# q and k loaded as runs of 18 tokens, with scores of 128 rows of contraction, and the first two weight tiles in two transfers ahead of v

## The chip, the cores and the metric

The kernel runs on one core of one Trainium2 chip. The core has TensorE (PE in the profile; its weight loads are PEld), VectorE (DVE), ScalarE (ACT), GpSimd (POOL) and SyncE (SP), and 16 DMA engines that all queues share. The metric is the time of one execution on the device in microseconds, the median over several executions.

## The reference

The inputs are q, k, v of shape (8, 8, 576, 64), that is batch, heads, tokens and head size, gates s of shape (8, 8, 576), and the weights w_r and w_i (64, 512, 512) and w_ch (512, 512), all in float32. First comes causal attention with a bias from the cumulative sum of the gates:

```
scores = q @ k.T / sqrt(64)
cum    = cumsum(max(s, 0))                      # along the tokens
scores = where(key after query, -1e9, scores + min(-(cum[query] - cum[key]), 0))
attn   = softmax(scores);   x = attn @ v        # heads side by side: (8, 576, 512)
```

Then a mixing of the first 64 frequencies along the tokens, with one complex 512x512 matrix to each frequency, and a last product:

```
X  = rfft(x, axis=tokens)
Yr = Xr[m] @ w_r[m] - Xi[m] @ w_i[m]
Yi = Xr[m] @ w_i[m] + Xi[m] @ w_r[m]            # m = 0 .. 63, zero above
u  = x + irfft(Y)
out = u + max(u @ w_ch, 0)
```

The two weight tensors hold 64 x 512 x 512 numbers each, 134 MB together, and each number is read once.

## The kernel before

**Work items.** The attention runs over N = 32 items. Item n is a pair of heads g = n // 8 (two of the eight heads) in a batch b = n % 8. A loop over n at the end of the attention part makes one pass for each item. In pass n, PE does in this order: the scores of head h = 0 of item n (`scores(n, 0)`), the second head's product of probabilities and v for item n - 1 (`av(n - 1, 1)`), the first part of the transposes of item n + 1 (`transposes(n + 1, 0)`), `scores(n, 1)`, `transposes(n + 1, 1)`, the forward transform of item n - 1 (`fft(n - 1)`), `av(n, 0)`, and the products with weight tiles that are due (`modes`). From pass 26 on, six passes also do parts of the last product ahead of time. The order is written out by hand; each engine takes its instructions in that order and waits on semaphores.

**Loads.** All loads of q, k, v and the weights go through POOL's queue, by `nc.gpsimd.dma_start` in `load` (L226), and turn float32 into 16 bits on the way. Eight semaphores serve POOL's transfers in turn, so each issue waits until the eighth transfer before it has landed. In pass n, `load` mixes the four transfers of item n + 3 (q, k, and v for two heads; `LA = 3`) with the weight transfers of this pass; each list is spread evenly over the pass. How many weight tiles a pass loads is planned ahead (`on_chip`), so that a tile is only loaded into a buffer whose last use was in an earlier pass. A weight tile covers 4 frequencies by 128 rows by 512 columns and is loaded by two transfers of 256 KB (at the destination), each to 64 of the 128 partitions, with runs of 2 KB. The first eight tiles lie in space that is used for something else later (`early`); the rest go round two rings of 11 and 6 buffers. Counted over the passes, passes 12, 14, 16, 20, 26 and 28 load no or one weight tile, most others 4 or 5.

**q and k.** A tile of q holds both heads of an item. Its 128 partitions are (head, 64 groups), and a group is a run of R = 9 tokens of 64 numbers: 2304 B at the source, 1152 B at the destination. k has a tile of its own. Each pool entry is one item; there are four (`bufs=LA + 1`).

**Transposes.** `transposes(n, 0)` turns q of item n and `transposes(n, 1)` turns k. Each makes 18 PE transposes of 64x64 (9 token positions, two heads) into one PSUM tile `tr_ps`, of which there is one. Head 0 comes out on partitions 0 to 63 and head 1 on 64 to 127. Two copies (L336) take them to SBUF: `qtA`, `qtB` by DVE; `ktA` by DVE and `ktB` by ACT. Tiles A have 65 rows (64 of the head and one for the cumulative sum of the gates, row 64 of q against a row of ones in k). Tiles B have 128 rows: the extra row is row 0, rows 1 to 63 are zeros, and the head is in rows 64 to 127. There are two sets, for even and odd items. SP brings the row of cumulative sums of each item and head (`cum_rows`, two small transfers an item).

**Scores.** For each head and each of two key residues, PE writes the causal mask into PSUM (L368), adds keys times queries (L374; contraction over 65 rows for h = 0, over 128 for h = 1), and ACT takes the exponential (L382). The last 64 tokens are handled for both heads together in `scores4` (L345, L349).

**Start.** Before the loop, SP loads s, two constants and, a little later, three more constants; POOL loads q and k of item 0, and then three weight tiles mixed with v of item 0, the last 64 tokens' v (`loads_tails`), and q, k, v of item 1. DVE sets the fixed rows of the tiles, casts the identity and the mask, and makes the cumulative sums; PE's first transposes come after that.

**End.** After the loop, `loads_w(len(wq))` issues the remaining weight tiles. PE multiplies each as it lands (L452), with parts of the last product between. After the last tile come the inverse transform, the last product, and the results' way out.

## Time and profile before

| What | Value |
|---|---|
| median of 6 executions | 447.95 us (447.44 to 448.89) |
| the profiled execution's own time | 448.01 us |
| its span, first to last instruction | 446.1 us |
| PE busy | 357.6 us (80%) |
| POOL busy | 259.8 us (58%) |
| DVE busy | 251.3 us (56%) |
| ACT busy | 218.7 us (49%) |
| DMA packets | 77251, 93.30 MB, mean 209 GB/s |
| q transfers | 32 of 144 KB, median 7.2 us to landing |
| k transfers | 32 of 144 KB, median 7.0 us to landing |
| v transfers | 72 of 64 KB, median 6.9 us to landing |
| weight transfers | of 256 KB, median 8.0 us to landing |

How to read it: the profile shows one execution. The page cuts the span into 40 slices of 11.15 us; in each slice a digit is the busy share of an engine in tenths, PEclk is TensorE's granted clock in tenths of full speed, and GB/s counts the bytes at the destination of the transfers. Most loads read 4 bytes and write 2, so what is read from HBM is nearly twice that. The chain that ended last is followed back from the last instruction, at each step to what released it. A wait line names who waited, for whom, and then the total in microseconds, how many times, and the longest. A timeline line has the start, the time it took, the engine, line and operation, and in brackets the idle time before it with what ended that. A window line has the stretch, its length, each engine's busy time with the number of instructions, the granted clock, the DMA engines' share and GB/s. The share sums the packets' own times, and since packets of one engine overlap, a full stretch shows more than 1.

### The profile page before, as it was taken

The page shows a single profiled execution, that of the slowest core. Times are in us where ns is not written, and L with a number is a line of the kernel's source. Part 1 is how long each engine was busy: PE and PEld are TensorE (multiplying, and loading weights), DVE is VectorE, ACT ScalarE, POOL GpSimd, SP SyncE. Part 2 cuts the span into 40 slices and gives each one's busy share as a digit, 9 for nine tenths or more (in the row PEclk, how much of TensorE's full clock was granted, in tenths as well). Part 3 has the DMA queues.
Part 4 walks back from the last instruction along what each step waited for, and adds up shares of the span by engine and source line. Part 5 has one row for each costly group of instructions (what it writes and reads, how often), then busy time and mean ns, then how long its engine had stood idle before and what let it go on. Part 6 is the DMA issues. An engine that isn't in the chain of part 4 may idle for free.

```text
span 446.1 us, 11492 instructions
## 1 busy us (share of the span) xinstructions
PE 357.6 (80%) x4729; PEld 222.5 (50%) x4729; DVE 251.3 (56%) x576; ACT 218.7 (49%) x387; POOL 259.8 (58%) x405
## 2 busy tenths in 40 slices
PE   1788998998476989957868976779987997769994
PEld 0466665566244666634545544546654555333341
DVE  6777676477243476644436455446665554441885
ACT  1486876177224474734436345556550344221583
POOL 7866765755566666555565656566543544440393
PEclk9999998699665699986669869889998899979999
DMA  9999999999999999999999999999999999996598
GB/s 178 199 203 205 205 202 206 201 207 206 207 207 203 195 190 199 208 207 207 206 200 206 207 207 206 208 205 203 206 210 211 209 210 209 209 217 131 173 351 346
DMA packets 77251, 93.30 MB, mean 209 GB/s; under 512 B 30144, under 2 KB 39872, under 8 KB 77200
## 3 DMA queue, kind: packets, MB, share of 16 engines
q0 software_dynamic: 67984, 81.29, 105.4%
q1 hardware_dynamic: 9216, 11.29, 7.8%
q8 instruction: 37, 0.61, 0.5%
q14 instruction: 14, 0.11, 0.1%
HBM read 163.51 MB, written 9.44 MB: 388 GB/s over the span
## 4 chain that ended last, share of the span: by engine, by line
DMA 68%; PE 14%; issue 6%; POOL 6%; DVE 4%; POOLq 1%; ACT 0%; DVEq 0%
DMA w_sb<-in_moe_w_i_dram 38%; DMA w_sb<-in_moe_w_r_dram 14%; DMA q<-in_q_dram 8%; PE sc_ps L374 3%; POOL r_w L766 3%; PE av_ps L403 2%; PE ft_ps L429 2%; PE sc_ps L368 2%; PE tr_ps L333 2%; DMA wch_sb<-in_moe_w_ch_dram 2%; DMA y_acc<-in_moe_w_r_dram 2%; DMA v<-in_v_dram 2%; DMA y_acc<-in_moe_w_i_dram 1%; DMA x_all<-in_moe_w_r_dram 1%; PE yp L452 1%
## 5 line engine op out<-in xcount | busy, mean ns | idle before, releaser
L382 ACT ACTIVATE p_sb<-sc_ps,cumt_sb 128x576 f16<-128x576 f32 (+1 forms) x256 | 142.0, 636 | 60.5 <-PE sc_ps L374 60.0
L226 POOL DMA_DIRECT2D w_sb<-in_moe_w_r_dram x120 | 71.6, 597 | 59.5 <-DMA w_sb<-in_moe_w_r_dram 19.8
L226 POOL DMA_DIRECT2D w_sb<-in_moe_w_i_dram x120 | 71.3, 596 | 46.9 <-DMA w_sb<-in_moe_w_i_dram 15.4
L226 POOL DMA_DIRECT2D v<-in_v_dram x72 | 51.7, 719 | 25.3 <-DMA w_sb<-in_moe_w_i_dram 7.5
L368 PE MATMUL sc_ps<-negm,ident 128*128 128x256 bf16 x256 | 56.1, 305 | 0.2
L452 PE MATMUL yp<-w_sb,xs 128*32 128x512 bf16 (+1 forms) x480 | 43.3, 441 | 9.4 <-DMA w_sb<-in_moe_w_i_dram 2.8
L333 PE MATMUL tr_ps<-ident,q 64*64 64x64 bf16 x576 | 17.0, 208 | 35.9 <-DMA q<-in_q_dram 35.9
L403 PE MATMUL av_ps<-v,p_sb 128*128 128x65 f16 x1024 | 44.9, 199 | 0.0
L374 PE MATMUL sc_ps<-qtB,ktB 128*128 128x512 bf16 (+2 forms) x192 | 43.6, 344 | 0.0
L336 DVE COPY ktA<-tr_ps 64x576 bf16<-64x576 bf16 x32 | 24.0, 749 | 33.0 <-PE tr_ps L333 33.0
L336 DVE COPY qtA<-tr_ps 64x576 bf16<-64x576 bf16 x32 | 23.8, 744 | 31.9 <-PE tr_ps L333 31.8
L403 PEld LDWEIGHTS <-p_sb 128*128 128x128 f16 x1024 | 39.0, 101 | 5.3 <-DVE x_all L413 2.3
L353 ACT ACTIVATE p<-sc_ps,cumt 128x64 f16<-128x64 f32 x32 | 10.1, 314 | 56.1 <-PE sc_ps L349 56.1
L374 PE MATMUL sc_ps<-qtA,ktA 65*128 65x512 bf16 (+2 forms) x192 | 37.1, 303 | 0.6 <-DMA qtA<-ncum_sb 0.6
L439 DVE CAST xs<-ft_ps 64x128 bf16<-64x128 f32 x128 | 31.4, 284 | 9.3 <-PE ft_ps L429 8.8
L429 PE MATMUL ft_ps<-Ff_sb,x_all 128*64 128x96 f16 (+1 forms) x640 | 34.1, 229 | 1.0 <-DVE x_all L413 1.0
L408 DVE TENSOR_REDUCE den<-av_ps 128x5 f32<-128x10 f32 x64 | 10.8, 169 | 41.6 <-PE av_ps L403 40.8
L452 PEld LDWEIGHTS <-xs 128*32 128x32 bf16 (+1 forms) x512 | 19.7, 146 | 27.7 <-issue 17.6
L413 DVE TENSOR_TENSOR x_all<-av_ps,rcp 128x320 f16<-128x320 f32 x64 | 31.5, 492 | 2.2
L333 PEld LDWEIGHTS <-q 64*64 64x64 bf16 x576 | 13.2, 120 | 38.5 <-DMA q<-in_q_dram 37.3
L336 ACT COPY ktB<-tr_ps 64x576 bf16<-64x576 bf16 x32 | 20.3, 634 | 22.2 <-DVE ktA L336 21.2
L333 PE MATMUL tr_ps<-ident,k 64*64 64x64 bf16 x576 | 16.9, 206 | 16.9 <-DVE qtB L336 8.1
(119 smaller groups left out, 558.7 us busy)
## 6 DMA issues: line engine op xcount, KB each, us to landing
w_sb<-in_moe_w_r_dram POOLq DMA_DIRECT2D x120, 256.0 KB, 8.0
w_sb<-in_moe_w_i_dram POOLq DMA_DIRECT2D x117, 256.0 KB, 8.1
out_dram<-r_w SPq DMA_DIRECT2D x14, 512.0 KB, 2.9
q<-in_q_dram POOLq DMA_DIRECT2D x32, 144.0 KB, 7.2
k<-in_k_dram POOLq DMA_DIRECT2D x32, 144.0 KB, 7.0
v<-in_v_dram POOLq DMA_DIRECT2D x72, 64.0 KB, 6.9
x_all<-in_moe_w_i_dram POOLq DMA_DIRECT2D x6, 256.0 KB, 6.8
out_dram<-r_w SPq DMA_DIRECT2D x6, 256.0 KB, 3.2
```

What stands on the lines that cost most here:

```text
L226: nc.gpsimd.dma_start(out=dst, in_=src)
L333: nc.tensor.transpose(ps[rows, r, :], src[rows, r, :], ident16[rows, rows])
L336: copy(out=dst[n % NQ][rows, :].rearrange("d (p r) -> d p r", r=R), in_=ps[rows].rearrange("d r p -> d p r"),)
L368: nc.tensor.matmul(ps[:, bass.ds(w * S, W)], ident16, negm[:, bass.ts(r, W)], start=True, stop=False, skip_group_check=True,)
L374: nc.tensor.matmul(ps[:, c0 : c0 + i1 - i0], keys[:, w, r, :], qt[:, i0:i1], start=False, stop=True, skip_group_check=True,)
L382: nc.scalar.activation(out=pt[:, poff[x] : poff[x] + S - w * W], in_=ps[:, w * S : (w + 1) * S - w * W], func=ACTF.Exp, bias=cumt_sb[:, x, ...
L403: nc.tensor.matmul(ps[:, I, r : r + NCH], lhsT, rhs, start=(i == 0), stop=(i == len(todo) - 1), skip_group_check=True,)
L413: nc.vector.tensor_tensor(out=x_all[:, g, b, :, D * h : D * h + D], in0=ps[:, :, 1 : NCH], in1=rcp.unsqueeze(2).to_broadcast([P, NT, D]), ...
L429: nc.tensor.matmul(ps[HP * h : HP * h + HP, q_, :], x_all[:nT, g, b, T, q_::2], Ff_sb[:nT, T, 3 * HM * h : 3 * HM * (h + 1)], start=(T == ...
L439: nc.vector.tensor_copy(out=xs[g % 2][rows, :, k, h, :, b, :], in_=ps[rows, :, k * HM : (k + 2) * HM].rearrange("p q (r m) -> p q r m", r=2),)
L452: nc.tensor.matmul(ps[32 * cg : 32 * cg + 32, :], cols[k0:, q_, 1 - ri, :, c * MC // 2 + cg], wt[(g, c, ri, cg // 2)][k0:, 2 * (cg % 2) + ...
L766: nc.gpsimd.tensor_tensor(out=rs[i], in0=rs[i], in1=z1s[i], op=ALU.add)
```

## The change

**q and k.** A run is now R = 18 tokens (RP = 32 groups), 4608 B at the source and 2304 B at the destination. One tile holds q on partitions 0 to 63 (two heads of 32 groups) and k on partitions 64 to 127, for two items, n and n + 1 (batches b and b + 1). One transfer brings q of both items and another k of both; for items 0 and 1 there is a transfer for each. There are two pool entries of two items. `loads_qk(n + LA)` is called in odd passes only, for items n + 3 and n + 4; `loads_v(n + LA)` in every pass.

**Transposes and tiles.** `transposes(n, half)` takes 9 of the 18 token positions of q and of k together, again in 18 PE transposes of 64x64. q comes out on rows 0 to 63 and k on rows 64 to 127, for both heads. The copies go to `qt` and `kt`, which have 128 rows and both heads side by side: 64 rows of the head, row 64 for the cumulative sum (ones in `kt`), and zeros below. DVE makes three of the four copies of an item and ACT the second half of k. The copies now write pieces of 9 elements and leave out 9.

**Scores.** Both heads contract over 128 rows.

**Start.** The first two weight tiles, which lie side by side, are loaded by two transfers of 512 KB at the destination (1 MB at the source) that stand between q and k of item 0 and v of item 0. The third weight tile is mixed with v of item 0, q and k of item 1, v of item 1 and the tails.

The diff, cut to its core:

```diff
-    R = S // (P // 2)
-    RP = P // 2
+    RP = P // 4
+    R = S // RP
+    RH = R // 2
...
-    qkpool = at.enter_context(tc.tile_pool(name="qk_sb", bufs=LA + 1))
+    qkpool = at.enter_context(tc.tile_pool(name="qk_sb", bufs=2))
...
-    qtA = [ap_.tile([NCH, S], BF16, name=f"qtA{i}") for i in range(NQ)]
-    qtB = [ap_.tile([P, S], BF16, name=f"qtB{i}") for i in range(NQ)]
+    qt = [ap_.tile([P, 2, S], BF16, name=f"qt{i}") for i in range(NQ)]
...
-    def loads_qkv(n):
+    def loads_qk(n):
...
-        q2 = qkpool.tile([P, R + 1, D], BF16, name="q2", tag="q2")[:, :R, :]
-        k2 = qkpool.tile([P, R + 1, D], BF16, name="k2", tag="k2")[:, :R, :]
+        t = loaded[n] = loaded[n + 1] = qkpool.tile([P, 2, R * D], BF16, name="qk2", tag="qk2")
+        return [
+            (
+                t[HP * i : HP * i + HP, x0:x1],
+                src[b + x0 : b + x1, hs].rearrange("b h (p r) d -> (h p) b (r d)", r=R),
+            )
+            for x0, x1 in ([(0, 2)] if n else [(0, 1), (1, 2)])
+            for i, src in enumerate((q, k))
         ]
...
+    def loads_v(n):
...
     def loads_w(upto):
         todo = []
+        if not wt:
+            t = y_acc[:, 2:6, :].rearrange("p c e -> p (c e)").bitcast(BF16)
+            for i in range(2):
+                wt[wq[i]] = early[i]
+            for h in range(2):
+                todo.append((
+                    t[HP * h : HP * h + HP].rearrange("p (m q e) -> p m (q e)", q=2, e=DM),
+                    moe_w_r[h : MC : 2, :P, :].rearrange("m (p q) e -> p m (q e)", q=2),
+                ))
...
-    first, second, tails0 = loads_qkv(0), loads_qkv(1), loads_tails(0)
+    first = loads_qk(0)
     load(first[:2])
-    load(loads_w(W0), first[2:] + tails0 + second)
+    load(loads_w(2))
+    load(loads_v(0) + first[2:] + loads_v(1) + loads_tails(0), loads_w(W0))
...
-        nc.vector.memset(qtB[i][0:64, :], 0.0)
-        nc.vector.memset(ktB[i][0:64, :], 0.0)
-        nc.vector.memset(ktB[i][0:1, :], 1.0)
-        nc.vector.memset(ktA[i][D : D + 1, :], 1.0)
+        nc.vector.memset(qt[i][D:], 0.0)
+        nc.vector.memset(kt[i][D:], 0.0)
+        nc.vector.memset(kt[i][D : D + 1], 1.0)
...
-        nc.sync.dma_start(out=qtA[n % NQ][D : D + 1, :], in_=ncum_sb[p0 : p0 + 1, :])
-        nc.sync.dma_start(out=qtB[n % NQ][0:1, :], in_=ncum_sb[p0 + 1 : p0 + 2, :])
+        for h in range(2):
+            nc.sync.dma_start(out=qt[n % NQ][D : D + 1, h, :], in_=ncum_sb[p0 + h : p0 + h + 1, :])
...
-    def transposes(n, which):
+    def transposes(n, half):
...
+        src = loaded[n][:, n % 2, :].rearrange("p (r d) -> p r d", d=D)[:, half * RH : half * RH + RH]
+        ps = trpool.tile([P, RH, 2 * RP], BF16, name="tr_ps", tag="tr")
+        for r in range(RH):
+            for i in range(2):
+                rows = slice(HP * i, HP * i + HP)
                 nc.tensor.transpose(ps[rows, r, :], src[rows, r, :], ident16[rows, rows])
...
+        for i, dst in enumerate((qt, kt)):
+            copy = (nc.vector.tensor_copy, nc.scalar.copy)[half * i]
+            to = dst[n % NQ][:D].rearrange("d h (p r) -> d h p r", r=R)
             copy(
+                out=to[:, :, :, half * RH : half * RH + RH],
+                in_=ps[HP * i : HP * i + HP].rearrange("d r (h p) -> d h p r", h=2),
             )
...
-            load(loads_qkv(n + LA) + tails_due, loads_w(on_chip[n]))
+            load((loads_qk(n + LA) if n % 2 else []) + loads_v(n + LA) + tails_due, loads_w(on_chip[n]))
```

## The prediction

> **What bounds the kernel now**
>
> I read the page's slices first, then the chain that ended last, then what PE and POOL wait for, and last the DMA traffic of single stretches.
>
> ```profile
> span 446.1 us, 11492 instructions
> ...
> PEclk9999998699665699986669869889998899979999
> DMA  9999999999999999999999999999999999996598
> GB/s 178 199 203 205 205 202 206 201 207 206 207 207 203 195 190 199 208 207 207 206 200 206 207 207 206 208 205 203 206 210 211 209 210 209 209 217 131 173 351 346
> ...
> DMA 68%; PE 14%; issue 6%; POOL 6%; DVE 4%; POOLq 1%; ACT 0%; DVEq 0%
> ```
>
> The DMA engines are full from the first slice to the 36th. In the end stretch the chain, in order of time, is one DMA after another, and then PE with the last product of the weight matrices:
>
> ```profile
> 399.43 10.42 DMA w_sb<-in_moe_w_i_dram
> 409.88 0.66 PE yp L452 x4
> ```
>
> So the span is a transfer stream of 409.9 us and a tail of 36.2 us (446.1 - 409.9) which needs the last weights and holds nothing that the change touches. A change to the attention's compute is worth nothing by itself; one to the stream counts in full. PE stands waiting for q, so it has time to give away:
>
> ```profile
> PE tr_ps L333 <- DMA q<-in_q_dram: 37.9, 14, 5.7
> ...
> POOL w_sb L226 <- DMA w_sb<-in_moe_w_r_dram: 32.4, 57, 1.2
> ```
>
> What a packet costs follows from two stretches in which the engines are equally full, 330 to 395 us (weights alone) and then 175 to 315 us (weights, q, k, v):
>
> ```profile
> DMA packets 7562, 13.67 MB, mean 210 GB/s; under 512 B 860, under 2 KB 988, under 8 KB 7556
> ...
> q0 software_dynamic: 7380, 13.42, 110.8%
> ```
>
> ```profile
> DMA packets 25494, 28.75 MB, mean 205 GB/s; under 512 B 10761, under 2 KB 14601, under 8 KB 25477
> ...
> q0 software_dynamic: 24645, 28.48, 118.2%
> ```
>
> 16 engines x 65 us = 7562 a + 13.67 MB b, and 16 x 140 us = 25494 a + 28.75 MB b, give a = 5.5 ns for a packet and b = 73 ns for 1000 B. The stretch of 20 to 70 us (10777 packets, 10.19 MB) with the first gives a = 4.8 ns. I take 5.2 ns. The packets' own times (the shares in the queue lines) solve the same way to 22.5 ns and 73.5 ns per 1000 B; most of the 22.5 ns lies beside the packet before.
>
> **The change, part by part**
>
> *q and k in runs of 18 tokens, two items to a transfer.* A run has 1152 B at its destination now and 2304 B after. Before: 64 transfers (32 q, 32 k) of 128 packets, 8192; after: 32 items x 2 x 64 rows = 4096, in 4 transfers for the first two items and 30 for the rest. With the weight tiles (4 transfers become 2) there are 32 transfers fewer; each carries 16 small packets (860 under 512 B in the first stretch, for 52 transfers), so 512 more go. The bytes stay. 4608 x 5.2 ns / 16 = 1.5 us off the stream. Ends: nothing of it, if a run of 4608 B at the source is cut in two (largest SWDGE packet seen: 2048 B, from 4096 B); 4608 x 22.5 ns / 16 = 6.5 us, if the whole own time went. I take 1.5, since the engines' shares of over 110% show the overlap.
>
> The page "DMA: Bandwidth & Descriptors" of the Trainium skill ("Why small descriptors are slow") puts a fixed cost of about 3 cycles on each packet and says that joining descriptors is only worth it at 256 B or less, which speaks against this change at 1152 B. At the 850 MHz which that page gives, 3 cycles are an estimated 3.5 ns, and the sum would be 1.0 us in place of 1.5. Its "Rules for kernel authors" also advise one 128-partition transfer over two half ones, and q and k now fill half the partitions each; by that rule nothing is gained there.
>
> No loss from half the partitions: every weight transfer fills 64, and those run at 210 GB/s.
>
> *The first weights in two transfers of 512 KB (at the destination), ahead of v.* The windows of the start:
>
> ```profile
> 2.00:3.00 1.00, 0.00 (x0) 0.00 (x0) 0.75 (x2) 0.24 (x2) 1.00 (x2) 1.00 0.88 160
> 3.00:4.00 1.00, 0.00 (x0) 0.00 (x0) 0.81 (x3) 0.00 (x0) 1.00 (x3) 1.00 0.75 109
> 4.00:5.00 1.00, 0.00 (x0) 0.00 (x0) 0.84 (x2) 0.00 (x0) 1.00 (x2) 1.00 1.05 283
> 5.00:6.00 1.00, 0.00 (x0) 0.00 (x0) 0.52 (x16) 0.00 (x0) 1.00 (x3) 1.00 1.14 264
> ```
>
> The last two columns are the engines' share and GB/s. POOL is busy all the time, so its issuing (0.6 to 0.75 us each) keeps the engines short. Against the 1.22 of a full stretch, 0.34 + 0.47 + 0.17 + 0.08 are missing, 0.87 us of stream. The third issue was a v of 64 KB and is now 512 KB, so the gap closes from about 3.2 us on. I take 0.3 of 0 to 0.87. v of item 0 lands later, but av(0, 0) starts at 21.2 us.
>
> *POOL's queue.* 32 issues of some 0.57 us fewer, 18 us; nothing gained, as POOL waits for landings of earlier transfers (each issue waits for the eighth before it). Where POOL rests 2 us with small transfers in flight, the stream thins (160 to 165 us: 174 GB/s; 145 to 150: 185); larger transfers in flight could save 0.3 there, even items with only v behind them could lose as much: 0.
>
> *PE.* As many transposes (36 an item, 64x64) and matmuls. The h = 0 matmuls go from 65 rows to 128: the means are 303 ns (65 rows) and 344 (128), the medians 298 and 300, so most of this is the clock they met. At most 192 x 41 ns = 7.9 us of PE, under the 37.9 us that it waits for q.
>
> *DVE and ACT.* Four copies an item as before (744 to 749 ns on DVE, 634 on ACT), written in pieces of 9 elements instead of rows; 64x576 elements each. Between no change and twice the time (three copies on DVE: +2.2 us an item, DVE then at 323 of 446 us), still under the DMA; I take none. All scores now need the ACT copy, which h = 0 did not: for item 2 it ended at 28.41 and the first score product began at 28.75, cover 0.34 us; without it PE loses a part of its waiting. Memsets at the start: 1.2 us more (64x576 words for 64x288 at 0.30 us, four times), under DVE's waits of 0.42 and 1.07 us for the identity and the mask.
>
> *SP.* The same two rows of cumulative sums an item, now into one tile; nothing else is queued there in the attention.
>
> *The wait that is moved.* The first half's transposes of an even item now need q and k, not q alone; an odd item's are on chip already. For item 28, q was issued at 275.41 and k at 279.70, and PE took q at 282.91 and k at 287.63. With k's landing 1.4 us later (two transfers of double size, 144 KB more each at 206 GB/s) the first transposes come at 289.0, the second 2.6 later at 291.6: PE is 4.0 us late in this item, and gets 2.05 back at the next, where it waited for q. Queued behind are PE's scores, av and modes, and POOL waits for the weight buffers that modes frees. The closest such pairs, modes(...) of passes 14 and 16 and POOL's first weight load of passes 15 and 17:
>
> ```profile
> 151.12 1.94 PE L452 MATMUL yp<-w_sb,xs 128*32 128x512 bf16 x16
> ...
> 159.20 0.60 POOL L226 DMA_DIRECT2D w_sb<-in_moe_w_r_dram  x1 [0.46 <-issue]
> ...
> 167.11 2.98 PE L452 MATMUL yp<-w_sb,xs 128*32 128x512 bf16 x32 [0.36 <-DVE xs L439]
> ...
> 175.41 0.60 POOL L226 DMA_DIRECT2D w_sb<-in_moe_w_r_dram  x1 [0.75 <-PE tr_ps L333]
> ```
>
> Slack 159.20 - 153.06 = 6.1 and 175.41 - 170.09 = 5.3 us, over the 4.0; behind it lie eight transfers in flight (8.0 us to landing). Cost: none.
>
> *Sum.* -1.5 - 0.3 = -1.8 us: the span goes to 444.3, and the profiled execution's 448.01 to 446.2. It is 0.06 above the median of 447.95, so no further correction.
>
> **The rivals**
>
> 1. *Runs cut in two.* Against it: a run from HBM to a 2304 B row passes whole on SP's queue; for it: no SWDGE packet over 2048 B is in the trace. Then only the start and 512 small packets (0.2 us) remain: 447.95 - 0.5 = 447.5, the same.
> 2. *The stream runs dry (slower).* PE's later k makes weight buffers come free late in passes 15 and 17 of the loop. For it: PEclk falls to 5 after long waits (115 to 155 us), and the waits grow as two are merged; a PE at half clock takes some 4 us longer an item. It decides when PE is late by more than 5.3 us and the 8.0 us in flight have run out, 13.3 us; at two items of half clock (4.0 + 8.0 = 12.0) it just doesn't. If it is late by 16, 3 us go: 447.95 - 1.8 + 3 = 449.2. Against it: PE gets up to 5.7 us back at odd items.
> 3. *Packets cost their own time.* 6.5 us at most; halfway to it, (1.5 + 6.5)/2 + 0.3 = 4.3: 443.7. Against it: the shares over 110%.
>
> **How the numbers follow**
>
> Forecast 0.64 (own range 445.3 to 447.3), cut runs 0.17, dry stream 0.12, dearer packets 0.07. A time can be told from no change by about 0.2%, 0.9 us: 447.05 to 448.85 is the same. Faster: 0.58 of the forecast and 0.07, 0.65; same: 0.04 of the forecast and the cut runs' 0.17, 0.21; slower: 0.12 and 0.02, 0.14. The range 444.9 to 448.3 leaves out the dear packets (most of 0.07), the dry stream (0.12) and little else.
>
> **What would show it**
>
> Packets 77251 down to about 72640, none of them 1152 B; SWDGE packets of 2304 B; the last weight's landing at 408.1 (409.9 - 1.8), the tail still 36.2; the first slice above 178 GB/s; PE's waits at the transposes longer and fewer, now ended by k. About 76700 packets would mean rival 1; slices under 190 GB/s past 140 us, with POOL waiting for yp, rival 2. I am wrong if the tail moves by over 1 us, since I hold it fixed.

## The result, and the profile after

The changed kernel takes 447.14 us (median of 29 executions) where the kernel before takes 448.32 (66 executions measured beside it). The ratio of the two, worked out over their executions, is 0.9978, with a 95% interval of 0.9970 to 0.9985. It is faster by 1.0 us by this ratio (the medians alone lie 1.2 us apart); the forecast was a gain of 1.8. The profiled execution took 447.34 us; the kernel before's took 448.01. Two executions on record, one of the kernel before and the profiled one of split2 (below), took over 700 us and stand in no ratio.

The page of the changed kernel, span, slices, DMA traffic and the chain's shares by engine:

```profile
span 445.4 us, 11428 instructions
...
PEclk9998999997967869998596969689997798989998
DMA  8999999999999999999999999999999999996598
GB/s 182 199 206 206 204 206 204 207 208 207 207 209 202 205 205 186 207 207 209 206 198 206 208 207 206 208 204 203 201 209 210 211 211 208 209 217 124 177 352 336
DMA packets 72643, 93.30 MB, mean 209 GB/s; under 512 B 29632, under 2 KB 31168, under 8 KB 72592
...
DMA 45%; PE 32%; DVE 8%; POOL 6%; issue 4%; ACT 2%; POOLq 1%; DVEq 0%; ACTq 0%
```

There are 4608 packets fewer, as counted in the forecast (72640). The DMA engines are still full to the 36th slice. The rate at 145 to 178 us went from 195, 190 and 199 GB/s (slices 14 to 16 before) to 205, 205 and 186: one thin place is gone and another is new. The chain's shares name DMA less than before (45% for 68%). Since the engines are as full as before, I take that for the way the chain was followed back through PE's waits. Its end is the same:

```profile
397.87 10.99 DMA w_sb<-in_moe_w_i_dram
408.91 0.66 PE yp L466 x4
```

The last product starts at 408.91 where it started at 409.88, and the tail behind it is 445.4 - 408.9 = 36.5 us for 36.2. So in these two executions 0.97 us came off the stream and 0.3 us went back in the tail.

What PE waits for, and then what POOL waits for, in us in total, times, and longest:

```profile
PE tr_ps L346 <- DMA qk<-in_k_dram: 28.6, 8, 5.2
PE tr_ps L346 <- DMA qk<-in_q_dram: 22.6, 7, 10.4
```

```profile
POOL w_sb L241 <- DMA w_sb<-in_moe_w_r_dram: 30.4, 52, 1.5
...
POOL w_sb L241 <- PE yp L466: 14.3, 11, 2.4
```

and in the kernel before, beside its waits for q:

```profile
PE tr_ps L333 <- DMA k<-in_k_dram: 4.9, 6, 1.1
...
POOL w_sb L226 <- PE yp L452: 3.0, 5, 0.8
```

PE's waits for q and k at the transposes are fewer (15 for 20) and some longer, and k ends more of them than q. POOL's waits for yp, the products that free the weight buffers, were 3.0 us in five and are 14.3 us in eleven.

### The profile page after: what moved, and what is told of

Same layout as the page of the kernel before. It is cut to its first block, busy times and chain, and to the rows that moved or that the text cites. A ratio compares the mean times of both kernels' runs of the same rounds, so it can differ in the third digit from the quotient of the medians.

```text
span 445.4 us, 11428 instructions
## 1 busy us (share of the span) xinstructions
PE 346.7 (78%) x4729; PEld 219.8 (49%) x4729; DVE 251.3 (56%) x574; ACT 221.3 (50%) x387; POOL 241.4 (54%) x373
## 4 chain that ended last, share of the span: by engine, by line
DMA 45%; PE 32%; DVE 8%; POOL 6%; issue 4%; ACT 2%; POOLq 1%; DVEq 0%; ACTq 0%
DMA w_sb<-in_moe_w_i_dram 17%; DMA qk<-in_k_dram 12%; DMA w_sb<-in_moe_w_r_dram 10%; PE yp L466 5%; PE z_ps L638 4%; PE sc_ps L388 4%; PE av_ps L417 4%; PE ft_ps L443 3%; PE sc_ps L382 3%; POOL r_w L780 3%; PE tr_ps L346 3%; DMA y_acc<-in_moe_w_r_dram 2%; PE z_ps L549 2%; DMA x_all<-in_moe_w_r_dram 2%; DVE kt L350 2%
## 5 line engine op out<-in xcount | busy, mean ns | idle before, releaser
L350 DVE COPY qt<-tr_ps 64x576 bf16<-64x576 bf16 x64 | 47.8, 748 | 74.7 <-PE tr_ps L346 74.7
L346 PE MATMUL tr_ps<-ident,qk 64*64 64x64 bf16 x1152 | 35.3, 206 | 63.4 <-DMA qk<-in_k_dram 28.6
L388 PE MATMUL sc_ps<-qt,kt 128*128 128x512 bf16 (+2 forms) x384 | 77.7, 315 | 2.2 <-ACT kt L350 2.1
L346 PEld LDWEIGHTS <-qk 64*64 64x64 bf16 x1152 | 26.9, 118 | 73.8 <-DMA qk<-in_k_dram 29.6
L382 PE MATMUL sc_ps<-negm,ident 128*128 128x256 bf16 x256 | 54.5, 298 | 0.2
L388 PEld LDWEIGHTS <-kt 128*128 128x128 bf16 x384 | 40.5, 106 | 26.4 <-issue 5.5
L466 PE MATMUL yp<-w_sb,xs 128*32 128x512 bf16 (+1 forms) x480 | 38.6, 413 | 6.9 <-DVE yv L698 1.9
L350 ACT COPY kt<-tr_ps 64x576 bf16<-64x576 bf16 x32 | 23.0, 718 | 15.6 <-DVE qt L350 14.9
L443 PEld LDWEIGHTS <-x_all 128*64 128x64 f16 (+1 forms) x640 | 22.5, 113 | 9.0 <-DVE x_all L427 1.1
L638 PE MATMUL z_ps<-wch_sb,xs 128*128 128x512 f16 x96 | 25.0, 407 | 0.2 <-DVE xs L632 0.2
```

Of the source, the lines that this page charges most:

```text
L346: nc.tensor.transpose(ps[rows, r, :], src[rows, r, :], ident16[rows, rows])
L350: copy(out=to[:, :, :, half * RH : half * RH + RH], in_=ps[HP * i : HP * i + HP].rearrange("d r (h p) -> d h p r", h=2),)
L382: nc.tensor.matmul(ps[:, bass.ds(w * S, W)], ident16, negm[:, bass.ts(r, W)], start=True, stop=False, skip_group_check=True,)
L388: nc.tensor.matmul(ps[:, c0 : c0 + i1 - i0], keys[:, w, r, :], qh[:, i0:i1], start=False, stop=True, skip_group_check=True,)
L443: nc.tensor.matmul(ps[HP * h : HP * h + HP, q_, :], x_all[:nT, g, b, T, q_::2], Ff_sb[:nT, T, 3 * HM * h : 3 * HM * (h + 1)], start=(T == ...
L466: nc.tensor.matmul(ps[32 * cg : 32 * cg + 32, :], cols[k0:, q_, 1 - ri, :, c * MC // 2 + cg], wt[(g, c, ri, cg // 2)][k0:, 2 * (cg % 2) + ...
```

## Experiments

Theories at the outset. **A**: the change gains by packets alone, a packet is cheaper than the forecast's 5.2 ns, and the new start is worth nothing. **B**: the packet price was right, the start gives its 0.3 us, and about 0.6 us is lost because two items' loads come in one burst and PE is late. Two more came up on the way. **D**: the size and number of transfers counts by itself, beyond the packets. **E**: the new layout or its compute costs something.

Every run was measured beside the kernel before on the same chip. R: runs of 18 tokens with the new layout; M: two items in a transfer; S: the new start.

| run | holds | ratio | 95% interval | span, one execution |
|---|---|---|---|---|
| start_only | S | 1.0022 | 1.0005 to 1.0039 | 446.1 |
| runs_only, again | R, M | 0.9974, 0.9973 | 0.9957 to 0.9990, 0.9959 to 0.9986 | 445.0, 446.8 |
| one_item | R, S | 1.0014 | 0.9996 to 1.0031 | 445.7 |
| after_again | R, M, S | 0.9976 | 0.9962 to 0.9991 | 446.3 |
| runs_one, again | R | 1.0001, 0.9999 | 0.9985 to 1.0017, 0.9987 to 1.0011 | 446.0, 448.2 |
| pairs9, again | M | 0.9991, 1.0001 | 0.9979 to 1.0004, 0.9992 to 1.0010 | 445.9, 447.0 |
| split2 | R in 2 pieces | 1.0009 | 0.9998 to 1.0020 | |
| split3 | R in 3 pieces, S | 1.0068 | 1.0044 to 1.0091 | 447.5 |
| split6 | R in 6 pieces, S | 1.0112 | 1.0091 to 1.0132 | 450.1 |
| heads | R, a transfer a head | 1.0365 | 1.0348 to 1.0382 | 461.3 |
| k128 | 128 rows in scores only | 1.0006 | 0.9988 to 1.0025 | 445.9 |
| qk_first | R, M, S, order | 0.9966 | 0.9949 to 0.9982 | 444.5 |
| wch18 | R, M, S, wch later | 0.9975 | 0.9963 to 0.9987 | 444.0 |
| runs_qk_first | R, M, order | 0.9962 | 0.9947 to 0.9977 | 444.9 |
| best | R, M, order, wch later | 0.9963 | 0.9951 to 0.9976 | 443.6 |

Spans of single executions of one kernel differ by 0.9 us (the changed kernel: 445.4 and 446.3) to 2.2 us (runs_one), so verdicts go by the ratios. The intervals of split3, split6 and heads rest on 5 to 7 executions, the others on 11 or more.

### The start apart from the runs

**start_only** is the kernel before with the new start alone:

```diff
-    load(loads_w(W0), first[2:] + tails0 + second)
+    load(loads_w(2))
+    load(first[2:] + second + tails0, loads_w(W0))
```

(and the two 512 KB transfers in loads_w, as in the change).

> Only the new start on the kernel before: the first two weight tiles in two transfers ahead of v of item 0, q and k as before. Theory A (the packets were priced a little too high and the start is worth nothing, since DMA share and GB/s from 2 to 10 us are no higher in the changed kernel): ratio to before 0.9997 to 1.0003. Theory B (the start gives its 0.3 us and something else takes 0.6 us away later): 0.9993.

**runs_only** is the changed kernel with the old start:

```diff
-    load(loads_w(2))
-    load(loads_v(0) + first[2:] + loads_v(1) + loads_tails(0), loads_w(W0))
+    load(loads_w(W0), loads_v(0) + loads_tails(0) + first[2:] + loads_v(1))
```

> Everything of the change but the start: q and k in runs of 18 tokens, two items to a transfer, weights and v mixed at the start as before. Theory A: 4096 data packets and 480 small ones fewer at some 4.3 ns, 1.2 us, ratio 0.9973, the same as the whole change (0.9978). Theory B: the whole change less its 0.3 us of the start, 0.9985.

> Longer runs and merged transfers, old start, once more: 0.9974 if the two together gain what neither does alone; 0.9985 to 0.9995 if the first measurement was a low one and the parts simply add.

> The changed kernel as it is, beside the others on the same chip. Any theory: 0.9978 again (interval of the first 0.9970 to 0.9985). It says how far a repetition moves: if it stands outside 0.9965 to 0.9990, differences of 0.001 between these kernels mean nothing.

The start gains nothing: alone it costs 1.0 us (0.2 to 1.7), and with it the change stands at 0.9978 and 0.9976, without it at 0.9974 and 0.9973. In start_only's profile the loss lies in the second and third slice, 189 and 198 GB/s where the kernel before has 199 and 203: 11.15 x (10 + 5) / 205 = 0.8 us. The windows of the start, changed kernel (the last two columns are the engines' share and GB/s):

```profile
2.00:3.00 1.00, 0.00 (x0) 0.00 (x0) 0.70 (x2) 0.24 (x2) 1.00 (x2) 1.00 1.26 184
3.00:4.00 1.00, 0.00 (x0) 0.00 (x0) 0.93 (x2) 0.00 (x0) 1.00 (x3) 1.00 0.57 106
4.00:5.00 1.00, 0.00 (x0) 0.00 (x0) 0.67 (x2) 0.00 (x0) 1.00 (x2) 1.00 1.08 247
5.00:6.00 1.00, 0.00 (x0) 0.00 (x0) 0.96 (x1) 0.00 (x0) 1.00 (x3) 1.00 1.04 322
6.00:10.00 4.00, 0.63 (x4) 0.55 (x4) 3.81 (x23) 0.00 (x0) 1.45 (x3) 1.00 1.15 224
```

and the kernel before, the last of them:

```profile
6.00:10.00 4.00, 0.01 (x1) 0.02 (x1) 2.80 (x6) 0.00 (x0) 2.30 (x4) 1.00 1.28 238
```

The gap at 3 to 4 us is as deep as before (106 GB/s for 109), and POOL is still busy issuing all of it. What 2 to 3 and 5 to 6 us gain, 4 to 5 us (247 GB/s for 283) and 6 to 10 us give back: 224 GB/s for 238, with POOL busy 1.45 us for 2.30. Its next issues wait 2.83 us (to 10.29) and 2.28 us (to 13.28) for y_acc, the new 512 KB transfers. The first slice did rise from 178 to 182 GB/s, as the prediction asked for, but runs_one, which has the old start, shows 182 and 180: that sign tells nothing.

### Bursts, and PE late

**one_item** is the changed kernel with one transfer of q and one of k for each item, in every pass, four buffers:

```diff
-        t = loaded[n] = loaded[n + 1] = qkpool.tile([P, 2, R * D], BF16, name="qk2", tag="qk2")
+        t = loaded[n] = qkpool.tile([P, R * D], BF16, name="qk2", tag="qk2")
...
-            load((loads_qk(n + LA) if n % 2 else []) + loads_v(n + LA) + tails_due, loads_w(on_chip[n]))
+            load(loads_qk(n + LA) + loads_v(n + LA) + tails_due, loads_w(on_chip[n]))
```

> The changed kernel with a transfer of q and one of k for each item in each pass, in runs of 18 tokens still: 4096 data packets as in the changed kernel, 30 transfers more (480 small packets, 0.13 to 0.16 us). PE gets q and k of each item in its own pass, as before. Theory A: slower than the changed kernel by 0.1 to 0.2 us, ratio 0.9981. Theory B (bringing two items at once makes PE late, so that weight buffers come free late and the stream thins, 0.6 us lost): faster than the changed kernel by 0.4, ratio 0.997; POOL's waits for the products yp (14.3 us in the changed kernel, 3.0 before) fall back to about 3.

**qk_first** is the changed kernel with q and k of two items issued back to back at the start of odd passes:

```diff
-            load((loads_qk(n + LA) if n % 2 else []) + loads_v(n + LA) + tails_due, loads_w(on_chip[n]))
+            load(loads_qk(n + LA) if n % 2 else [])
+            load(loads_v(n + LA) + tails_due, loads_w(on_chip[n]))
```

> The changed kernel with q and k of the two items issued one after the other at the start of each odd pass, ahead of the weights, in place of 2 to 5 us apart. PE gets k some 2 to 4 us earlier. Packets and bytes are the same. Theory A: no difference from the changed kernel, 0.9978. Theory B: PE is less late, the stream thins less, 0.997.

one_item speaks against B, and surprised A too. POOL's waits for yp fell from 14.3 to 2.5 us, and the kernel didn't get faster; it lost the whole gain (1.0014). But it also has 30 transfers more, so it doesn't settle B alone. In qk_first those waits fall to 4.2 us and the time by 0.0012, which is inside the intervals; two more kernels with this order follow below. At the two longest waits for yp in the changed kernel, 2.37 us up to 327.15 and 2.26 us up to 336.44, the stream stays full:

```profile
324.00:328.00 4.00, 2.82 (x28) 1.65 (x27) 2.91 (x7) 0.59 (x1) 1.44 (x3) 1.00 1.12 210
333.00:337.00 4.00, 3.55 (x46) 2.28 (x45) 2.85 (x9) 1.14 (x3) 1.35 (x3) 1.00 1.12 211
```

### The price of a packet

**split3** and **split6** are one_item with each run landing in three or six rows, a few spare bytes between them; split6:

```diff
-        t = loaded[n] = qkpool.tile([P, R * D], BF16, name="qk2", tag="qk2")
+        t = loaded[n] = qkpool.tile([P, 6, R // 6 * D + 16], BF16, name="qk2", tag="qk2")
...
-                t[HP * i : HP * i + HP],
-                src[b, hs].rearrange("h (p r) d -> (h p) (r d)", r=R),
+                t[HP * i : HP * i + HP, :, : R // 6 * D],
+                src[b, hs].rearrange("h (p c r) d -> (h p) c (r d)", c=6, r=R // 6),
```

> The kernel of one_item (one transfer of q and one of k for each item, runs of 18 tokens), with each run landing in three rows of 768 B in place of one of 2304 B: 8192 packets more, the same bytes, the same issues; a few spare bytes between the rows, nothing else. It prices a packet by itself. Theory A (a packet costs the stream about 4.4 ns, less than the forecast's 5.2, and that is why the change won less): 8192 x 4.4 ns / 16 = 2.25 us more than one_item, 1.0014 + 0.0050 = 1.0064 of the kernel before. Theory B (the packet price of 5.2 ns was right and something else took back the gain): 2.66 us more, 1.0073. A packet that costs its own time of 22.5 ns: 11.5 us more, 1.027. Nothing for a packet: 1.0014. A and B lie 0.4 us apart here, so this run alone only rules out the far ends.

> The kernel of one_item with each run of q and k landing in six rows of 384 B: 20480 packets more than one_item, the same bytes and issues. Theory A (4.4 ns): 5.63 us more than one_item, ratio 1.0014 + 0.0126 = 1.0140. Theory B (5.2 ns): 6.66 us more, 1.0163. Own time (22.5 ns): 28.8 us, 1.066. With the run of three rows it gives a slope: the difference between the two, 12288 packets, is 3.4 us by A and 4.0 us by B. If POOL's rests (one of 2 to 3 us for each 900 or so packets of an engine) cost the stream a lot each, 1280 packets an engine more bring one or two rests more, and the slope is steeper than the trace's price.

The traffic of one_item and of split6:

```profile
DMA packets 73123, 93.30 MB, mean 209 GB/s; under 512 B 30112, under 2 KB 31648, under 8 KB 73072
```

```profile
DMA packets 93603, 93.30 MB, mean 207 GB/s; under 512 B 54688, under 2 KB 56224, under 8 KB 93552
```

20480 packets more, and the same bytes, cost 1.0112 - 1.0014 = 0.0098 (give or take 0.0027), 4.4 us: 4.4 x 16 / 20480 = 3.4 ns a packet, between 2.5 and 4.4. split3 alone gives 4.7 ns, give or take 2.6. The forecast's 5.2 ns is outside the first, and a packet's own 22.5 ns is far out. At 3.4 ns the 4608 packets that the change takes away come to 4608 x 3.4 / 16 = 1.0 us. That carries a price from pieces of 384 B over to runs of 1152 and 2304 B, and split6 has one rest of POOL more than the others (see the last section), which may be part of its 4.4 us.

3.4 ns stands near the 3 cycles that the page "DMA: Bandwidth & Descriptors" of the Trainium skill gives ("Why small descriptors are slow"), put in the prediction at an estimated 3.5 ns. Its advice that joining is only worth it at 256 B or less doesn't fit split3 and split6: pieces of 768 and 384 B, both larger, cost 2.4 and 4.4 us against whole runs of 2304 B. At 1152 B, the size of this change, no run decides it (split2 below).

### One thin place

From the trace of the changed kernel, windows at 170 to 180 us, and then POOL's timeline there:

```profile
170.00:175.00 5.00, 5.00 (x77) 3.24 (x75) 2.57 (x6) 2.21 (x4) 2.28 (x4) 1.00 1.17 186
175.00:180.00 5.00, 4.54 (x83) 3.11 (x84) 4.15 (x11) 3.13 (x6) 3.36 (x6) 1.00 1.20 179
```

```profile
168.85 0.71 POOL L241 DMA_DIRECT2D v<-in_v_dram  x1 [0.80 <-DMA qk<-in_k_dram]
170.64 0.70 POOL L241 DMA_DIRECT2D v<-in_v_dram  x1 [1.07 <-DMA w_sb<-in_moe_w_i_dram]
173.42 0.77 POOL L587 DMA_DIRECT2D wch_sb<-in_moe_w_ch_dram  x1 [2.08 <-issue]
```

POOL rests 2.08 us with two v of 64 KB behind it, and the rate falls to 186 and 179 GB/s; against 206 that is some 5 x (20 + 27) / 206 = 1.1 us of stream. **wch18** is the changed kernel with wch loaded two passes later:

```diff
-            if n == N // 2:
+            if n == N // 2 + 2:
                 nc.gpsimd.dma_start(out=wch_sb, in_=moe_w_ch.rearrange("(dt p) e -> p dt e", p=P))
```

> The changed kernel with the load of wch (512 KB) issued at the end of pass 18 in place of pass 16, nothing else. It tells what the dry stretch at 170 to 180 us (186 and 179 GB/s) is worth: there POOL rested 2.08 us after two v of 64 KB each and before wch. Theory C (where one of POOL's rests meets small transfers, the stream loses up to 1 us, and this took part of the gain): the rest now comes ahead of w_sb and qk that are issued anyway, with the same two v before it, so the stretch stays thin (about 185 GB/s); what changes is that wch's 512 KB no longer hold up the fifth and eighth weight behind it (1.99 us of waiting for wch at 180.35 us): up to 0.5 us gained, ratio 0.9967 to 0.9978. Theory A (packets alone): no change, 0.9978. If the place of wch was itself the trouble, the slice at 170 to 180 us goes to 200 GB/s and the gain is 1 us, 0.9956.

Its windows there:

```profile
170.00:175.00 5.00, 4.49 (x76) 2.97 (x71) 3.35 (x7) 3.44 (x7) 2.49 (x4) 1.00 1.25 200
175.00:180.00 5.00, 4.95 (x106) 3.67 (x104) 3.22 (x10) 3.11 (x7) 3.31 (x6) 1.00 1.17 197
```

The thin place is nearly gone, and that one execution's span is 444.0 us. The median doesn't follow: 0.9975, the changed kernel's ratio. What a thin place in one profiled execution would be worth by arithmetic was not what this kernel won over many.

### Longer runs and merged transfers, singly

**pairs9** is the kernel before with two items to a transfer (q2 and k2 as [P, 2, R * D], loads at odd passes as in the change), runs of 9 tokens, old layout and compute. **runs_one** is one_item with the old start.

> The kernel before with q and k of two items in one transfer (as in the change), but still in runs of 9 tokens (1152 B) on 128 partitions, in their own tiles, the old compute and the old start: 30 transfers and 480 small packets fewer. Theory A (packets alone, at the 3.4 ns that the spans of split3 and split6 give against one_item): 480 x 3.4 / 16 = 0.1 us, ratio 0.9998. Theory D (it is the merging of two items into one transfer, with fewer issues and more bytes behind each of the transfers in flight, that gains; the changed kernel was 0.0036 below one_item, which differs in that alone): 0.9964 to 0.9975. If merging makes PE late and costs instead: above 1.0010.

> The changed kernel with runs of 18 tokens, but one transfer of q and one of k for each item, and with the old start: 4096 packets fewer than before, the same number of issues. Theory A (packets alone): 4096 x 3.4 / 16 = 0.87 us, ratio 0.9981; at the forecast's 5.2 ns 1.33 us, 0.9970. Theory D (merging gains, longer runs do not show): 0.9992 to 1.0010, from one_item's 1.0014 less the 0.0004 to 0.0022 that the new start cost. Together with pairs9, runs_only (0.9974) and the kernel before it makes a table of two by two: by A the runs carry the gain, by D the merging.

> pairs9 once more. Theory A: 0.9998. Theory D: 0.9970 to 0.9991; in its first run the last weight landed about 1.1 us earlier than in the kernel before, but the tail behind it took 1.0 us longer in the profiled execution.

> runs_one once more, beside split2 and heads on the same chip. Theory A: 0.9981. Theory D and E: 1.0001 again.

Pooled over both runs, weighted by their intervals: longer runs alone 1.0000 (give or take 0.0010), merging alone 0.9998 (0.0007), both 0.9973 (0.0010). If the parts added, both would stand at 0.9998; they are 0.0024 below that, give or take 0.0016, 1.1 us. By the packet price longer runs alone should have gained 4096 x 3.4 / 16 = 0.9 us and gained nothing, while both together gained 1.2 us for the 1.0 of their packets. In whole times, neither A nor D says that.

Whole times are not the stream alone, however. In both profiled executions of pairs9 the last weight lands earlier than in the kernel before (408.5 and 409.6 us for 409.8), and the tail behind it takes 37.4 us for 36.2. The work in the tail is the same: the last store of the results is issued 32.05 us after the last product's start in both kernels. But that store takes 4.1 us to land where it took 2.9, and so do the larger ones before it. The stores of 512 KB in the kernel before, pairs9, the changed kernel and after_again, with the median time to landing in us:

```profile
out_dram<-r_w SPq DMA_DIRECT2D x14, 512.0 KB, 2.9
out_dram<-r_w SPq DMA_DIRECT2D x14, 512.0 KB, 4.1
out_dram<-r_w SPq DMA_DIRECT2D x14, 512.0 KB, 3.2
out_dram<-r_w SPq DMA_DIRECT2D x14, 512.0 KB, 3.5
```

If the stores take that long in all of pairs9's executions, merging alone shortens the stream by some 1.2 us (0.0027) and the stores give it back; then the table says nothing against parts that add. Two profiles don't show whether they do, nor why the stores differ.

Of runs_one the profile shows where it loses, in the windows of the same thin place:

```profile
170.00:175.00 5.00, 4.49 (x93) 3.26 (x92) 3.02 (x6) 4.68 (x10) 2.51 (x4) 1.00 1.19 200
175.00:180.00 5.00, 4.95 (x87) 3.56 (x88) 3.67 (x12) 2.87 (x5) 3.77 (x7) 1.00 1.10 156
```

156 GB/s for 5 us is about 1.2 us of stream, as much as its packets should bring. But runs_only, which does gain, has 161 GB/s in the same window, so this place alone is not the cause:

```profile
175.00:180.00 5.00, 4.66 (x95) 3.49 (x97) 3.41 (x10) 3.10 (x7) 4.01 (x7) 1.00 1.14 161
```

### Layout, compute, and the number of transfers

**split2** is runs_one with each run in two rows of 1152 B: the packets, issues and bytes of the kernel before, with the new layout. **k128** is the kernel before with 128 rows of contraction for the first head too:

```diff
-    qtA = [ap_.tile([NCH, S], BF16, name=f"qtA{i}") for i in range(NQ)]
+    qtA = [ap_.tile([P, S], BF16, name=f"qtA{i}") for i in range(NQ)]
...
+        nc.vector.memset(qtA[i][D:, :], 0.0)
+        nc.vector.memset(ktA[i][D:, :], 0.0)
```

(ktA likewise). **heads** is runs_one with a transfer for each head:

```diff
-                t[HP * i : HP * i + HP],
-                src[b, hs].rearrange("h (p r) d -> (h p) (r d)", r=R),
+                t[HP * i + RP * h : HP * i + RP * h + RP],
+                src[b, 2 * g + h].rearrange("(p r) d -> p (r d)", r=R),
             )
+            for h in range(2)
```

> The kernel of runs_one (new layout and compute, one transfer of q and one of k an item, old start) with each run landing in two rows of 1152 B: exactly the packets, the issues and the bytes of the kernel before; only the layout (64 partitions for q, 64 for k) and the compute on it differ. Theory A (packets alone count): 1.0000. Theory E (the new layout or compute costs 0.8 us and eats what the packets gain): 1.0018 to 1.0025, and runs_one stands 0.9 to 1.0 us below it (4096 packets at 3.4 to 4.0 ns). If longer runs gain nothing at all: 1.0000, the same as runs_one.

> The kernel before with 128 rows of contraction for the first head's scores (64 rows of data, one of cumulative sums or ones, the rest zeros), nothing else: no transfer, packet or issue changes. Theory A and the forecast (PE has 37.9 us of waiting to give away, so 192 products at up to 41 ns more cost nothing): 1.0000. Theory E (the compute of the new layout costs the 0.6 us that a fit over all runs gives to the layout): 1.0009 to 1.0014.

> The kernel of runs_one with one transfer for each head: 128 transfers of q and k in place of 64, 32 partitions and 72 KB each, the runs of 18 tokens unchanged; 1024 small packets more. Theory A (packets alone): 1024 x 4.0 / 16 = 0.26 us over runs_one, ratio 1.0007. Theory D (what counts is the number of issues, since each waits for the eighth before it and small ones leave the engines short of bytes: 30 issues fewer gained about 1.0 us, 0.033 us each): 64 more cost 2.1 us or more, 1.0047; POOL's waits for landings of earlier transfers grow and slices under 200 GB/s appear where q, k and v follow one another.

k128 shows no cost (1.0006, interval on both sides of 1), and E is neither shown nor excluded: split2's 1.0009 lies between no change and the 0.9 us that longer runs alone are missing. split2 against runs_one is also the direct price of this change's packets, 1152 against 2304 B with all else equal: 1.0009 - 1.0000, give or take 0.0015, or 0.4 us between -0.3 and 1.1. That holds both nothing and the 0.9 us.

heads is the clear one: 64 transfers more, with 1024 packets more (0.2 us by 3.4 ns), cost 16 us. POOL's timeline in heads, and the window at the rest:

```profile
178.56 0.50 POOL L232 DMA_DIRECT2D qk<-in_q_dram  x1
179.68 0.49 POOL L232 DMA_DIRECT2D qk<-in_k_dram  x1 [0.62 <-DMA w_sb<-in_moe_w_i_dram]
180.16 0.74 POOL L232 DMA_DIRECT2D v<-in_v_dram  x1
184.21 0.73 POOL L232 DMA_DIRECT2D v<-in_v_dram  x1 [3.31 <-PE ft_ps L433]
```

```profile
182.00:186.00 4.00, 3.54 (x76) 2.43 (x75) 3.16 (x9) 2.79 (x5) 1.79 (x3) 1.00 0.52 72
```

Four transfers of q and k of 72 KB and one v of 64 KB lie behind the rest of 3.31 us, 72 GB/s is moved for 4 us, and the engines stand half empty (0.52). The rests are not all of it: the rate also falls where POOL issues without a pause, eight transfers in 4 us, three of them of 72 KB.

```profile
166.00:170.00 4.00, 3.99 (x75) 3.05 (x76) 2.58 (x8) 2.79 (x6) 4.00 (x8) 0.90 1.02 138
```

So D holds in this direction: transfers of half the size cost far more than their packets, and at this rest the stream runs half empty. How much of the merged transfers' gain is such cover is not separated from the packets.

### A version faster than both

**runs_qk_first** is runs_only with qk_first's order; **best** adds wch18's move.

> The changed kernel without its new start (first weights as before the change) and with q and k of two items issued back to back at the start of odd passes. Both parts alone stood at 0.9974 and 0.9966 of the kernel before, against 0.9978 for the whole change. Theory A (start worth nothing or a loss of some 0.5 us, order of the loads worth 0.4): 0.9958 to 0.9966, 446.4 to 446.8 us at 448.3 for the kernel before. Theory B (the start is worth a gain of 0.3 us): 0.9973. If the differences among these are where dry stretches happen to fall, anything from 0.996 to 0.998.

> The changed kernel without its new start, with q and k first in odd passes, and with wch's load at the end of pass 18 in place of 16: the parts that each stood at or below the changed kernel. If they add (0.9962 for the first two, and in the profiled runs of wch18 against the changed kernel the slice of 170 to 180 us went from 186 to 203 GB/s, worth 0.8 to 1.0 us): 0.9940 to 0.9945. If the dry stretches only move elsewhere: 0.9960 as without the move of wch.

best beats the kernel before by 0.0037 (446.33 us for 448.15) and runs_qk_first by 0.0038 (446.67 for 447.93). Both stand some 0.0015 below the changed kernel, at the edge of the intervals. The page of best:

```profile
span 443.6 us, 11406 instructions
...
GB/s 181 202 206 206 204 205 205 208 207 208 207 207 205 206 203 206 207 207 208 205 202 208 207 206 199 207 207 205 208 209 211 210 210 209 210 216 124 175 353 345
```

No slice from the second to the 36th is under 199 GB/s. The parts don't add: wch's move gains nothing here either.

The order does show when runs are pooled. The three kernels with q and k first (qk_first, runs_qk_first, best) stand at 0.9963, the five measurements of R and M without it (the changed kernel twice, runs_only twice, wch18) at 0.9976. The difference is 0.0013, give or take 0.0010, 0.6 us. POOL's waits for yp are 4.2 to 6.2 us in the profiles of the three and 9.8 to 15.2 in those of the five. So what B says, that a late PE takes part of the gain, is not excluded, though the runs don't show that these waits are the reason.

## Why the prediction was right or wrong

The direction was right, the size was not: 1.0 us for 1.8. The step that failed is the size of the two terms that were counted, first of all the price of a packet.

- **"I take 5.2 ns" (packets, -1.5 us).** The count is right to three packets, and no run was cut: SWDGE packets of 2304 B are in the trace, median 192 ns (1152 B: 107). The price is the failed term: 3.4 ns (2.5 to 4.4) measured, 1.0 us in place of 1.5. It was fitted to two stretches that differ in more than packets, and all of the lower rate beside q, k and v was put on packets. With 3.4 ns the same two equations leave 20 us of engine time over, 1.3 us of the 140 us stretch; that thin places there (200 GB/s in slice 21) make up these 1.3 us is argued and not measured. heads shows that the rate can fall by much with hardly a packet more.
- **"I take 0.3 of 0 to 0.87" (start).** It gained nothing beside the rest of the change, and alone it lost 1.0 us. The step "the gap closes from about 3.2 us on" failed; the gap at 3 to 4 us stayed, and the larger transfers held POOL up behind 6 us, which the sum left out.
- **"Nothing gained" in POOL's queue, "larger transfers in flight could save 0.3".** In whole times merging alone gained nothing, but pairs9's slower stores may hide a gain. That size of transfer and length of run gain together what neither gains alone, as the whole times have it, was in no part of the sum, which only adds.
- **The moved wait, none.** The times came out: for item 28 the first half's transposes waited for k until 287.98 us and the second half's began at 291.84 (forecast 289.0 and 291.6). The cost of none is not shown. POOL's waits for yp grew to 14.3 us; the stream stayed full at the longest, and one_item, which has 2.5, was slower; yet the kernels with q and k first, with 4.2 to 6.2, gained 0.6 us more, give or take 0.4.
- **Half the partitions and 128 rows, none.** 128 rows alone: no cost that can be told. The layout: open (split2). The copies in pieces of 9 took as long as before on DVE (748 ns) and 718 ns for 634 on ACT.
- **The tail, fixed at 36.2 us.** It wasn't fixed. It was 36.5 us in the first profile, within the 1 us that the forecast allowed, but in after_again the last weight landed at 408.9 again and 37.4 us followed, 1.2 more than before: 0.6 because the last product waited for PE (last section) and 0.6 because the last stores landed later. Counted from the landing, that is over the 1 us which the prediction named as its sign of being wrong. So a change to the stream doesn't count in full: the 0.97 us that came off it left 0.7 us of the span in the first profile and nothing in the second (446.3 us for 446.1). The landing itself was forecast for 408.1.
- **Rivals.** Cut runs and packets at their own time are excluded by the trace and by split6. Both signs of the dry stream came, a slice under 190 GB/s past 140 us (186) and POOL waiting for yp, but not in one place: in the thin slice POOL waits for landings and rests, not for yp.

The two failed terms, 0.5 us of packets and 0.3 of the start, are as large as the 0.8 us that were missing. That the sum closes is not proof of it and may be luck: the table of two by two doesn't add in whole times, and the order of the loads and the tail move the time by as much.

**Open:** why longer runs alone gain nothing and, with merged transfers, 1.2 us. The thin place at 175 us, the layout's compute and the bursts were tried; none carries it by itself. How far the slower stores of pairs9 explain it, and what makes them slower, was not tried.

## What to carry to other kernels

Price a packet by adding packets to one transfer with all else equal, not by comparing two stretches of a trace: the stretches can differ in more than their packets. In a stream that is fed by one issuing engine, look first at what lies behind each of its rests; small transfers there can cost far more than their packets. Where a change has two parts that meet in one queue, measure each part and both before adding them up, and look in each profile where the time went: the part that you did not touch may differ too.

## What was unexpected in the hardware

- In each of the four kernels looked at, POOL rests 1 to 3.6 us whenever another 900 to 1000 packets of its queue (SWDGE packets in the prediction) have gone through each engine. By the packets that had started by the end of each rest: 983, 1937, 2859 and 3812 an engine in the kernel before (at 78, 163, 246 and 345 us), 971, 1886, 2834 and 3770 in the changed one (86, 173, 266, 378 us), 1003, 1975, 2928 and 3866 in heads. split6, with the most packets, has five: 969, 1898, 2801, 3725 and 4664 (59, 127, 183, 253 and 325 us). They are named after whatever else ended then, and the landing that POOL needed, of the eighth transfer before, was by then 1.7 to 3.2 us old. POOL has other waits as long, which end with a landing or with PE freeing a buffer. Fewer packets move the rests to later places in the program; what is in flight there seems to decide what a rest costs (72 GB/s at the second one in heads, 186 and 179 in the changed kernel). What causes them no run here shows.
- The last product of the weights doesn't always wait for the last landing. In after_again PE had a long stretch of work in order behind a wait of 2.00 us for weights, and a part of it ran at half the clock. PE's timeline there:

```profile
398.32 1.07 PE L466 MATMUL yp<-w_sb,xs 128*32 128x512 bf16 x6 [2.00 <-DMA w_sb<-in_moe_w_i_dram]
...
400.77 3.55 PE L638 MATMUL z_ps<-wch_sb,xs 128*128 128x512 f16 x8
...
409.54 0.65 PE L466 MATMUL yp<-w_sb,xs 128*32 128x512 bf16 x4
```

  and in the changed kernel's first profile:

```profile
401.19 2.22 PE L638 MATMUL z_ps<-wch_sb,xs 128*128 128x512 f16 x8
...
408.91 0.65 PE L466 MATMUL yp<-w_sb,xs 128*32 128x512 bf16 x4 [0.22 <-DMA w_sb<-in_moe_w_i_dram]
```

  The same eight products took 3.55 and 2.22 us, and in the first case the last product waited for PE alone. The clock granted to PE was 0.50 and 0.77 in the window around them (the column before the engines' share), first in after_again, then in the changed kernel's first profile:

```profile
400.00:404.00 4.00, 4.00 (x16) 1.62 (x14) 1.31 (x3) 0.59 (x1) 0.00 (x0) 0.50 1.12 210
400.00:404.00 4.00, 3.60 (x18) 1.51 (x16) 1.74 (x3) 0.59 (x1) 0.00 (x0) 0.77 1.13 217
```

  PE stood idle before the last product for 0.44 us before the change and for 0.22 after. By so little is the end of this kernel set by the stream, and executions fall on either side: in the profiles of runs_one (both), after_again, qk_first, runs_qk_first and heads PE had no idle time there, and the last product began up to 0.6 us after the landing.
